# A recurrent attention feeding an MLP: VectorE held to the program's order, weight pieces dealt anew, two turnings set apart

## The chip, the core and the metric

The kernel runs on one core of a Trainium2 chip. A core has several engines that run side by side, each with its own queue of instructions: TensorE (PE, matrix products; its weight loads are shown apart as PEld), VectorE (DVE, elementwise work), ScalarE (ACT, functions of one input and copies), GpSimd (POOL) and SyncE (SP), which here only issues DMAs. An engine works through its queue in order; an instruction whose inputs or buffers are not ready holds up all that stand behind it. The metric is the time of one execution on the device in microseconds (us).

## What is computed

The first half is a gated linear recurrence with 4 batches, 8 heads, 768 steps and a head size of 48. Its output, brought into token order, goes through an MLP with 3072 tokens, 384 in and out, 2048 within.

```python
f = 1.0 / (1.0 + np.exp(-f_logit))
for t in range(S):
    state = f[:, :, t, :, None] * state + np.einsum('bhd,bhe->bhde', k[:, :, t], v[:, :, t])
    y[:, :, t] = np.einsum('bhd,bhde->bhe', q[:, :, t], state)
x = y.transpose(0, 2, 1, 3).reshape(B * S, H * D)
h = x @ w_in
g = h * (1.0 / (1.0 + np.exp(-1.702 * h)))
return g @ w_out
```

## The kernel before

**Units.** The tokens are cut into 12 units of 256 (three to a batch). For each unit, the attention yields x for 256 tokens, and the MLP is run on these one to three units later, so that TensorE always has products of the MLP to do while VectorE and ScalarE prepare the next step of the attention.

**The attention of a unit** avoids the step-by-step loop by a tree: six levels of pairs of blocks within chunks of 64 tokens. A level needs scores (L384, bank "sc" of PSUM), masks put on them by VectorE (L410, "A"), products with the rows of v that belong to the level (L448, "y"), and a multiplication of q and k by the gates of the level (`promote`: L436 and L437 in units 0 to 2, one instruction at L439 from unit 3 on), after which ScalarE sets a half of q or k aside for the next level (L423, "Kc" and "Qc"). GpSimd makes the products of the gates (L376, "tot"). After the levels, k is turned (L505, "tkn", and its copy "kn" L506), the sums of k and v per chunk are formed (L523) and VectorE makes four states one after the other (L538, L540, L543, "st"). Then TensorE multiplies q by the states (L563), ScalarE copies the result out of PSUM ("yT", L571), and DMAs bring it to token order ("xT").

In units 0 to 2 a step handles one level (kind W, six steps), from unit 3 on two levels at once (kind V, three steps). The two turns of k are kind T, the states kind S.

**The beginning of the next unit** has four functions, called within the parts of the present unit: `begin_f` (turn the gate logits, make the sigmoid, load those of the unit after), `begin` (turn q, save its last column on GpSimd, load the next q), `begin_k` (turn k; from unit 3 on also the first copies and the first L439), `begin_gates` (the gate products on GpSimd). For units 0 to 2 a turn is made by TensorE and ScalarE (L339, L342); from unit 3 on by one VectorE instruction (L327), for f followed by the sigmoid on ScalarE. `parts_of` (L817) makes the list of a unit's parts and puts the beginnings of the next unit into it, as parts of kind B or K.

**The MLP.** A group h of 128 hidden columns is three matmuls over 256 tokens (L727); then come the sigmoid on ScalarE (L732) and g on VectorE (L733). There are 16 such groups per unit, in four blocks. The product with w_out is done plainly for units 0 to 2 (L755, added up at L791 and L793), and from unit 3 on by seven products of quarters instead of eight (L704, with banks X, W, Y, Z). For these, VectorE makes sums of quarters of g (L641, L643, L644, L650) and of w_out (L622, once), and combines the products (u, L679 to L691). Matmul results of h, o, and the turns share four banks of PSUM.

**The weights** arrive as bits of another format and are converted by VectorE. There are 32 pieces (half of w_in, half of w_out), and each takes one ScalarE instruction (L208) and five on VectorE (L223, L219, L226, L227, L228, on 128x384 each). `convert()` emits one such instruction. Three buffers hold fetched pairs of pieces; a fetch is issued by SyncE as soon as a pair is done.

**The order.** `merge(n, fill, columns, share, pieces, …)` writes out the order of the work for unit n. It goes through the parts of the unit; after each part it emits a share of MLP work from the list `fill` (shares W 3, V 4, S 3, T 1, B 1, K 1, out of their total, of `columns` columns of matmul in all), and spreads conversions between them until `pieces` pieces are dealt. `UNIT` is the MLP work of a unit, 24576 columns, `DM` is 384, `LAG` is 18 DM. Two scopes say which engines keep this order as written:

```python
ctx.enter_context(tc.manual_schedule(engines={mybir.EngineType.PE}))
fill_order = ExitStack()
fill_order.enter_context(tc.manual_schedule())
...
merge(3, fill, 3 * UNIT // 2 - LAG // 2, steady, 6, by=0.7)
fill_order.close()
```

Up to the end of merge(3) all engines keep the written order; after `fill_order.close()` only TensorE does, and a scheduler orders the instructions of the other engines when the kernel is built.

Of the kernel before, what the change touches and what calls it, by code (L numbers as in the profile page):

```python
# [23 lines left out]
def kernel(  # L24
# [34 lines left out]
    B, H, S, D = q.shape  # L59
    DM = H * D  # L60
# [25 lines left out]
    wp = ctx.enter_context(tc.tile_pool(name="wp", bufs=2))  # L86
    mlp = ctx.enter_context(tc.tile_pool(name="mlp", bufs=2))
    ps = ctx.enter_context(tc.tile_pool(name="ps", bufs=1, space=bass.MemoryType.PSUM))
    ctx.enter_context(tc.manual_schedule(engines={mybir.EngineType.PE}))
    fill_order = ExitStack()  # L90
    fill_order.enter_context(tc.manual_schedule())

# [138 lines left out]
    def convert():  # L231

        if state["begin"] < len(pairs) and len(todo) <= NOP:
            begin_pair(state["begin"])
            state["begin"] += 1
        if todo and todo[0]:
            todo.pop(0)()
        if todo and todo[0] is None:
            todo.pop(0)
            state["done"] += 2  # L240
            fetch_weights()
# [34 lines left out]
    def load_vl(n, l):  # L276

        if n >= NALL:
            return
        t = vls[n, l] = ld.tile([P, DM], F32, tag=f"vl{l}", name=f"vl_{n}_{l}")  # L280
        if n < N_TURN:
            pt = ps.tile([P, DM], F32, tag="mm", name=f"tv_{n}_{l}", bufs=4)
            for g in range(NG):
                nc.tensor.matmul(
                    pt[g * 64:(g + 1) * 64], lhsT=perm[:, l - 1, :] if l else ident[:, ::2], rhs=vns[n][:, g, :],
                    start=True, stop=True,
                )
            nc.scalar.copy(t, pt)
            return
        nc.sync.dma_start(out=t, in_=v_toks[n % 2].rearrange("(n two m) e -> two n m e", two=2, m=LEV[l])[0])  # L290
# [507 lines left out]
    def mlp_blocks(*blocks):  # L798

        hs, os = zip(*(mlp_block(n, r) for n, r in blocks))  # L800
        return sum(hs, []) + sum(os, [])


    def keep_up(times):

        if times:
            pt = ps.tile([P, NL * 64], F32, tag="mm", name=f"idle_{next(serial)}", bufs=4)
        for _ in range(times):
            nc.tensor.matmul(pt, lhsT=ident, rhs=masks.rearrange("p l t -> p (l t)"), start=True, stop=True)

    units = [attention(n) for n in range(NALL)]
    LAG = 18 * DM

    def parts_of(n):

        parts = list(units[n][1])
        _, inter = parts.pop()  # L817
        if n:
            kind, scores = parts[0]
            _, ahead = units[n - 1][1][-1]  # L820
            parts[0] = kind, lambda: (ahead(), scores())
        if n < N_TURN:

            def with_v(l):
                kind, fn = parts[l]
                return kind, lambda: (fn(), load_vl(n, l) if n == 0 or l else None, keep_up(2 * (n == 0 and l < 3)))
            parts[:NL] = [with_v(l) for l in range(NL)]
        if n + 1 < NALL:
            begin_f, begin, begin_k, begin_gates = units[n + 1][0]
            i = len(parts)  # L830
            if n + 1 < N_FILL:

                parts.append(("K", lambda: (begin_k(), begin_gates(), load_vl(n + 1, 0) if n + 1 < N_TURN else None)))
                parts.insert(i - 4, ("B", begin if n == 0 else lambda: None))
                parts.insert(i - 5, ("B", begin_f))
                if n:

                    kind, head = parts[0]
                    parts[0] = kind, lambda: (head(), begin())
            else:  # L840
                kind, states = parts.pop()
                parts += [("B", begin_k), (kind, lambda: (states(), begin_gates()))]
                parts.insert(i - 3, ("B", lambda: (begin_f(), begin())))
        else:
            parts.append(("W", inter))
        return parts

    def merge(n, fill, columns, share, pieces=0, hold=0, by=1.0, chores=()):

        parts = parts_of(n)
        total = sum(share(kind) for kind, _ in parts)
        converting = {"W": 3, "T": 3, "B": 1} if n < N_FILL - 1 else {"W": 3, "V": 4, "S": 3, "T": 1, "B": 1}
        total_ops = sum(converting.get(kind, 0) for kind, _ in parts)
        held = sum(share(kind) for kind, _ in parts[:hold])
        at = at_ops = done = ops = 0
        for kind, fn in parts:
            ready = state["done"]
            fn()  # L860
            for chore in chores[:2]:
                chore()
            chores = chores[2:]
            at += share(kind)
            at_ops += converting.get(kind, 0)
            n_ops = min(int(pieces * NOP * at_ops / (by * total_ops)), pieces * NOP) - ops
            ops += n_ops
            first, n_columns = done, max(0, columns * (at - held) / (total - held) - done)

            def some(end):  # L870
                nonlocal done
                while fill and done < end and fill[0][2] <= ready:
                    w, emit, _ = fill.pop(0)
                    emit()
                    done += w
            for i in range(n_ops):
                some(first + n_columns * i / n_ops)
                convert()
            some(first + n_columns)
# [4 lines left out]
    UNIT = NFF * NK * U + U // P * NFF * DM  # L884
# [12 lines left out]
        load_raw(1, j)  # L897
    load_vn(1)
    fill = []
    merge(0, fill, 0, steady, 8)  # L900
    fill += mlp_blocks((0, 0)) + mlp_blocks((0, 1))
    merge(1, fill, UNIT // 2 - LAG // 2, steady, 10, hold=1)
    fill += mlp_blocks((1, 0), (1, 1)) + mlp_blocks((0, 2), (1, 2))
    merge(2, fill, UNIT, steady, 8)
    fill += mlp_blocks((2, 0), (2, 1)) + mlp_blocks((2, 2), (0, 3)) + mlp_blocks((1, 3), (2, 3))
    merge(3, fill, 3 * UNIT // 2 - LAG // 2, steady, 6, by=0.7)
    fill_order.close()
    for n in range(3, NALL):
        fill += mlp_unit(n)
# [33 lines left out]
```

## Time and profile before

| | us |
|---|---|
| median of 13 runs | 655.84 |
| lowest and highest of them | 654.84, 658.31 |
| the profiled execution, its own time | 655.26 |
| span of that execution in the trace | 653.3 |
| TensorE busy in the span | 632.1 |
| VectorE busy | 445.0 |
| ScalarE busy | 229.9 |
| GpSimd busy | 60.1 |

The profile is of one execution. Its span runs from the first to the last instruction; the execution's own time holds 2.0 us more. TensorE's granted clock was at full speed throughout. Three kinds of view are used. Stage rows give, for a stretch of the span, the busy time of each engine, with the number of instructions in brackets, the granted clock, the mean share of the DMA engines and the rate. Waits give, for an instruction that waited, who released it, then the sum, the number of times, and the longest. Timeline rows give the start, the duration, the engine, the line, the operation, and output and input by the program's names, with their sizes and, in square brackets, the idle time before and its releaser. "x2" means two instructions in one row.

### The profile page before, as it was taken

The numbers are of one execution on the slowest core, as the hardware profiler recorded it, in microseconds if no ns is written. First come the engines' busy times: TensorE is split into PE (matmuls) and PEld (weight loads), VectorE is DVE, ScalarE is ACT, GpSimd is POOL, SyncE is SP. The second block draws the span as 40 slices with busy tenths as digits, with TensorE's granted clock in tenths as the row PEclk, the third lists the DMA queues.
The fourth block names the chain that finished last, engine by engine and source line by source line (L and its number), as shares of the span: only waits on it lengthen the run. The fifth ranks groups of instructions, "written<-read, shape, count | busy, mean of one in ns | idle before, by whom it ended". The sixth has DMA issues, their size and how long they took to land.

```text
span 653.3 us, 20397 instructions
## 1 busy us (share of the span) xinstructions
PE 632.1 (97%) x8958; PEld 541.8 (83%) x8958; DVE 445.0 (68%) x802; ACT 229.9 (35%) x477; POOL 60.1 (9%) x116
## 2 busy tenths in 40 slices
PE   6979999999999999999999999999999999999997
PEld 5656767767768789989989989989989889989997
DVE  2998977788787658558558558559559557553571
ACT  4464444333224324324324324334334333232120
POOL 3050020010001002002002002002002002000000
PEclk9999999999999999999999999999999999999999
DMA  8888874384044634604605605605604202101000
GB/s 193 220 206 214 219 162 122 105 201 79 25 93 122 168 72 121 166 27 122 165 25 129 160 26 128 159 26 130 158 27 108 63 25 64 38 2 26 25 1 24
DMA packets 67554, 67.67 MB, mean 104 GB/s; under 512 B 30410, under 2 KB 61290, under 8 KB 67466
## 3 DMA queue, kind: packets, MB, share of 16 engines
q1 hardware_dynamic: 67466, 66.38, 40.6%
q8 instruction: 70, 1.15, 0.8%
q14 instruction: 18, 0.15, 0.1%
HBM read 56.92 MB, written 8.65 MB: 100 GB/s over the span
## 4 chain that ended last, share of the span: by engine, by line
PE 86%; DVE 9%; ACT 2%; DMA 1%; issue 1%; SPq 1%; DVEq 0%; ACTq 0%
PE h L727 37%; PE o_Y L704 8%; PE o_X L704 7%; PE o L755 7%; PE o_Z L704 7%; PE sc L384 5%; PE y L448 4%; PE o_W L704 4%; PE t L339 2%; PE y L563 2%; PE sc L523 1%; PE tkn L505 1%; DMA xT<-yT 1%; DVE s L219 1%; DVE A L410 1%
## 5 line engine op out<-in xcount | busy, mean ns | idle before, releaser
L727 PE MATMUL h<-xT,w_in 128*128 128x256 f32 (+1 forms) x1152 | 259.8, 381 | 5.1 <-DMA xT<-yT 3.0
L727 PEld LDWEIGHTS h<-xT,w_in 128*128 128x128 f32 x1152 | 215.3, 190 | 38.6 <-issue 4.3
L733 DVE TENSOR_TENSOR g<-h,sg 128x256 f32<-128x256 f32 (+1 forms) x192 | 81.0, 423 | 97.8 <-ACT sg L732 95.4
L732 ACT ACTIVATE sg<-h 128x256 f32<-128x256 f32 (+1 forms) x192 | 73.5, 384 | 192.5 <-PE h L727 187.4
L423 ACT COPY Kc<-X 128x512 f32<-128x512 f32 x69 | 46.2, 669 | 119.3 <-DVE X L439 84.7
L755 PE MATMUL o<-w_out,g 128*128 128x384 f32 x192 | 66.1, 493 | 0.0
L439 DVE TENSOR_TENSOR X<-X,tot 128x1024 f32<-128x1024 f32 x45 | 55.1, 1225 | 15.4 <-PE sc L384 10.2
L755 PEld LDWEIGHTS o<-w_out,g 128*128 128x128 f32 x192 | 35.3, 190 | 22.9 <-issue 1.4
L704 PE MATMUL o_X<-w_out,g 128*128 128x192 f32 x288 | 51.9, 329 | 0.0
L704 PE MATMUL o_Y<-T,S 128*128 128x192 f32 x288 | 51.1, 331 | 0.1
L704 PEld LDWEIGHTS o_Y<-T,S 128*128 128x128 f32 x288 | 46.5, 190 | 2.6 <-DVE u L679 1.2
L704 PEld LDWEIGHTS o_X<-w_out,g 128*128 128x128 f32 x288 | 47.3, 190 | 0.9
L410 DVE TENSOR_TENSOR A<-sc,masks 128x512 f32<-128x512 f32 x72 | 46.8, 681 | 0.0
L376 POOL TENSOR_TENSOR tot<-F 128x512 f32<-128x512 f32 x12 | 12.5, 1042 | 342.3 <-DVE st L540 342.3
L448 PE MATMUL y<-A,vl 64*48 64x64 f32 x2304 | 41.2, 217 | 1.0 <-issue 0.6
L448 PEld LDWEIGHTS y<-A,vl 64*48 64x48 f32 x2304 | 36.2, 120 | 4.5 <-issue 3.8
L327 DVE STREAM_TRANSPOSE X<-raw 128x1024 f32<-128x1024 f32 x18 | 36.7, 2041 | 2.3 <-PE y L563 2.3
L571 ACT COPY yT<-y 48x512 f32<-48x512 f32 x48 | 27.8, 580 | 12.9 <-PE y L563 12.4
L384 PEld LDWEIGHTS sc<-X,Kc 48*64 48x64 f32 x1344 | 24.0, 134 | 8.9 <-issue 3.2
L384 PE MATMUL sc<-X,Kc 48*64 48x64 f32 x1344 | 28.3, 220 | 2.5 <-DVE A L410 2.1
L376 POOL TENSOR_TENSOR tot<-tot 128x256 f32<-128x256 f32 (+4 forms) x60 | 27.4, 457 | 4.7
L357 POOL COPY q_last<-X 128x4 f32<-128x4 f32 x12 | 14.0, 1166 | 141.2 <-DVE X L327 111.3
(93 smaller groups left out, 674.7 us busy)
## 6 DMA issues: line engine op xcount, KB each, us to landing
vl<-v_tok SPq DMA_DIRECT2D x60, 192.0 KB, 3.0
bits<-in_moe_w_out_dram SPq DMA_DIRECT2D x8, 768.0 KB, 10.1
bits<-in_moe_w_in_dram SPq DMA_DIRECT2D x8, 576.0 KB, 8.2
v_tok<-in_v_dram SPq DMA_DIRECT2D x10, 384.0 KB, 4.3
vn<-v_tok SPq DMA_DIRECT2D x10, 384.0 KB, 6.9
xT<-yT SPq DMA_DIRECT2D x24, 144.0 KB, 2.8
raw<-in_q_dram SPq DMA_DIRECT2D x18, 192.0 KB, 3.9
raw<-in_f_logit_dram SPq DMA_DIRECT2D x18, 192.0 KB, 4.7
```

Of the source, the lines that this page charges most:

```text
L327: nc.vector.transpose(out.rearrange("p (a i j) -> p a j i", a=NP, j=R), raw[:, j].rearrange("p a (j d) -> p (a j) d", j=R)[:, :, :32],)
L376: nc.gpsimd.tensor_tensor(tn, t2[:, :, 0], t2[:, :, 1], ALU.mult)
L384: nc.tensor.matmul(out[g * HS:(g + 1) * HS, h, a, :], lhsT=lhs(h, a * U + g * G), rhs=rhs(h, a * U + g * G), start=True, stop=True,)
L410: nc.vector.tensor_tensor(A[:, :, c:c + w].rearrange("p h (x t) -> p h x t", t=64), t["sc"][:, :, c:c + w].rearrange("p h (x t) -> p h x t ...
L423: nc.scalar.copy(c.rearrange("p (n m) -> p n m", m=m), X[:, j, :NA].rearrange("p (n two m) -> p n two m", two=2, m=m)[:, :, hf, :],)
L439: nc.vector.tensor_tensor(qk, qk, by, ALU.mult)
L448: nc.tensor.matmul(dst(h, g, a), lhsT=vls[n, u][g * 64:(g + 1) * 64, (2 * a + h) * D:(2 * a + h + 1) * D], rhs=A(h, g, a), start=(start an ...
L704: nc.tensor.matmul(t[bank], lhsT=lhs(f), rhs=rhs(f), start=(new and f == 0), stop=(f == HF - 1), skip_group_check=True,)
L727: nc.tensor.matmul(ph, lhsT=w_in[:, c, ff * P:(ff + 1) * P], rhs=xTs[n][:, c, :], start=(c == 0), stop=(c == NK - 1))
L732: nc.scalar.activation(sg, ph, AF.Sigmoid, scale=1.702)
L733: nc.vector.tensor_tensor(g[ff // FG][:, ff % FG, :], ph, sg, ALU.mult)
L755: nc.tensor.matmul(t["po"], lhsT=g[ff // FG][:, ff % FG, tt * P:(tt + 1) * P], rhs=w_out[:, ff, :], start=(ff == ffs[0]), stop=(ff == ffs[ ...
```

## The change

Four things are changed.

1. VectorE joins TensorE in the scope that lasts for the whole kernel: after merge(3) its instructions too stand in the order in which the program writes them. ScalarE, GpSimd and SyncE are ordered by the scheduler after merge(3), as they were.
2. From the third merge on (merges 2 to 10, where the next unit is 3 or later), `begin_f` and `begin` are no longer one part. `begin_f` stays where it was, and `begin` becomes a part of its own two places later. The total of the shares in those merges grows by one.
3. The pieces of weights dealt to merges 0 to 3 are 6, 10, 9, 7 instead of 8, 10, 8, 6. Their sum stays 32.
4. merge(1) gets 3·DM = 1152 columns of MLP work less, and merge(3) 1152 more.

```diff
-    ctx.enter_context(tc.manual_schedule(engines={mybir.EngineType.PE}))
+    ctx.enter_context(tc.manual_schedule(engines={mybir.EngineType.PE, mybir.EngineType.DVE}))
...
                 parts += [("B", begin_k), (kind, lambda: (states(), begin_gates()))]
-                parts.insert(i - 3, ("B", lambda: (begin_f(), begin())))
+                parts.insert(i - 3, ("B", begin_f))
+                parts.insert(i - 1, ("B", begin))
...
-    merge(0, fill, 0, steady, 8)
+    merge(0, fill, 0, steady, 6)
     fill += mlp_blocks((0, 0)) + mlp_blocks((0, 1))
-    merge(1, fill, UNIT // 2 - LAG // 2, steady, 10, hold=1)
+    merge(1, fill, UNIT // 2 - LAG // 2 - 3 * DM, steady, 10, hold=1)
     fill += mlp_blocks((1, 0), (1, 1)) + mlp_blocks((0, 2), (1, 2))
-    merge(2, fill, UNIT, steady, 8)
+    merge(2, fill, UNIT, steady, 9)
     fill += mlp_blocks((2, 0), (2, 1)) + mlp_blocks((2, 2), (0, 3)) + mlp_blocks((1, 3), (2, 3))
-    merge(3, fill, 3 * UNIT // 2 - LAG // 2, steady, 6, by=0.7)
+    merge(3, fill, 3 * UNIT // 2 - LAG // 2 + 3 * DM, steady, 7, by=0.7)
     fill_order.close()
```

The number of instructions on each engine stays the same.

## The prediction

> **What bounds the kernel now.** I read first the totals and the forty slices, then busy time by stage, then the waits, then the timeline at one hand-over between units.
>
> ```profile
> PE 632.1 (97%) x8958; PEld 541.8 (83%) x8958; DVE 445.0 (68%) x802; ACT 229.9 (35%) x477; POOL 60.1 (9%) x116
> PE   6979999999999999999999999999999999999997
> DVE  2998977788787658558558558559559557553571
> ```
>
> TensorE works 632.1 of 653.3 us, and the change takes no matmul away. So all that can be won is in its 21.2 us of idle time, and VectorE's row says where: it is full only in the first slices.
>
> ```profile
> core 0: us, PE busy (x) PEld busy (x) DVE busy (x) ACT busy (x) POOL busy (x), PEclk, DMA share, GB/s
> 0.00:56.00 56.00, 43.48 (x962) 32.72 (x964) 40.71 (x96) 27.91 (x50) 16.08 (x38) 1.00 0.84 200
> 56.00:93.00 37.00, 35.45 (x606) 24.77 (x603) 35.01 (x80) 18.52 (x37) 3.64 (x6) 1.00 0.87 214
> 93.00:158.00 65.00, 61.35 (x729) 45.06 (x731) 51.79 (x103) 22.73 (x48) 3.75 (x8) 1.00 0.56 131
> 158.00:246.00 88.00, 88.00 (x1048) 68.11 (x1041) 62.17 (x105) 28.02 (x60) 5.08 (x10) 1.00 0.36 94
> 246.00:600.00 354.00, 353.93 (x5363) 325.17 (x5362) 230.75 (x373) 124.48 (x261) 31.52 (x54) 1.00 0.34 87
> ```
>
> The rows are, in turn, unit 0; unit 1; unit 2 with the start of unit 3; the rest of unit 3 with unit 4; seven steady units. Idle TensorE by subtraction: 12.5, 1.6, 3.7, 0.0, 0.1, and 3.4 in the tail that is left out. From 158 us on there is nothing to win and something to lose: the gain must come out of the first 158 us. The waits name the small ones there, and two that already exist in steady units:
>
> ```profile
> PE h L727 <- DMA xT<-yT: 3.0, 3, 1.3
> PE h L727 <- ACT kn L506: 1.3, 1, 1.3
> PE y L563 <- DVE st L543: 1.2, 3, 0.5
> DVE X L439 <- ACT Qc L423: 6.1, 7, 1.5
> ```
>
> Columns: sum, times, longest. The last two say that the state sums (st) are sometimes just late for TensorE, and that the second score step waits for ScalarE's copies.
>
> **The change part by part.** Counts of instructions stay: order and timing change. The granted clock is 1.00 in every row, so I take all durations as they are.
>
> *Six pieces for eight in unit 0.* A piece costs five VectorE instructions (L223 0.37, L219 0.555, L226 0.35, L227 0.55, L228 0.55 us each; in back-to-back pairs they take about 0.27 and 0.47). Ten instructions fewer are 3.9 to 4.7 us of VectorE, which runs without a break from 13 to 45 us. But the level chain (L436, ScalarE's copy 0.66, scores 0.65, next L436) can't go faster than about 2.2 us a level. Dealing 3, 3, 4, 5, 4 conversions to levels instead of 4, 5, 4, 7, 6, and 10 instead of 14 ahead of the states, I get the states at 38.4 where the trace has them at 41.5: **−3.1 us** at the end of unit 0. If TensorE's own turns of k and v decide instead, −2.3.
>
> *Ten pieces in unit 1, with 1152 columns of MLP less.* The row 56 to 93 shows VectorE full: 35.0 of 37, and 57.4 to 83.9 with 0.6 us of gap. All 50 conversions remain; only one product g (0.42) leaves the stretch ahead of the states. TensorE, however, has two groups of h fewer there (2 × 1.295 = 2.6 us), so it now waits for about 2.2 us. The two groups come back after the states' scores, where they cover the 1.3 us wait for xT in the waits above. At the first h of unit 1 (trace: 92.5 us) I have 90.5, with the same TensorE work done: of −3.1, **−2.0 us** is left.
>
> *Nine pieces for eight and seven for six in units 2 and 3; 1152 columns more in unit 3.* Row 93 to 158 has VectorE at 80%; 10 instructions more at 0.4 are 4 us beside 13 of gap. The small stalls of TensorE at h there (xT 0.47, the sums 0.33, and 0.51 where a g stands behind two sums of w_out, L622, that the scheduler had pulled in) go, but the scores of unit 3 ask for more work in front of them. At those scores (sc of the second pair of levels) I have 37.5 us after h_8 of unit 0's last block, before 37.4: **+0.1**, between −1.2 and +1.5.
>
> *VectorE in program order from unit 3 on.* L622 (7.4 us in all) falls back behind the mark among g_9 to g_11, where TensorE has h in hand; its cost is the delay of one g: **+0.1**. In the tail of unit 3 the turning of F stands between g_12 and g_13: 2.05 us in which no bank of h comes free, with three banks ahead: 0 to 0.9, I take **+0.4**.
>
> *Turnings of f and q.* Today they run right after the states, in the gap before the score steps:
>
> ```profile
> 254.72 2.05 DVE L327 STREAM_TRANSPOSE F<-raw 128x1024 f32<-128x1024 f32 x1 [0.83 <-POOL tot L376]
> 256.62 1.29 DVE L650 TENSOR_TENSOR g<-g,S 128x512 f32<-128x512 f32 x2
> 258.28 2.06 DVE L327 STREAM_TRANSPOSE X<-raw 128x1024 f32<-128x1024 f32 x1 [0.37 <-PE y L563]
> 260.45 1.20 DVE L439 TENSOR_TENSOR X<-X,tot 128x1024 f32<-128x1024 f32 x1
> 261.58 1.27 DVE L410 TENSOR_TENSOR A<-sc,masks 128x512 f32<-128x512 f32 x2
> 263.02 1.24 DVE L439 TENSOR_TENSOR X<-X,tot 128x1024 f32<-128x1024 f32 x1 [0.18 <-ACT Qc L423]
> ```
>
> In the program's order they stand a whole unit's h later: f after g_8, q behind the sums that follow g_11, k after g_14. So the place above becomes free (4.1 us less ahead of L439), and 6 us of turning is put among the products. Behind the f-turning on VectorE wait g_9 and, on ScalarE, sg_10 (behind F's sigmoid, 1.06); TensorE waits for those only when four banks of h are filled. The raw loads on SyncE's queue, and POOL's two q_last copies (L357, 1.17 mean), are issued as much later and are still a unit ahead of use; POOL's own order is the same, as is that of SyncE's outputs; one w_out fetch goes behind an xT transfer, not ahead of it.
>
> Walked from h_8's end at 28.2 us after a score step: f turned 28.97 to 30.85, sigmoid to 32.0, q turned 35.2 to 37.1, k turned from 38.7 (behind g_14), first L439 step 41.45, g_15 42.6, two sums, states 44.4 to **47.5**. TensorE by its own work needs the states at 47.82. So the unit still fits, with about **0.3 us of slack**, where today the turnings are out of this chain altogether. The other place: after the scores, the copies yT (2.37 after y) hold ScalarE's Kc and Qc, so the second L439 starts 2.95 after the scores, u is ready at 6.9, and TensorE wants it at 6.7: 0.22, today 0.04 to 0.27. Score starts move two h-groups earlier (a share of 4/20 for 4/19 of the columns), behind which o_X and o_Y give cover. Starts of y in the trace at 257.16, 306.00, 403.32, 452.07, 500.68, 549.45 give 48.72 us a unit; I get 48.7 to 48.9. I take **0** for the seven hand-overs (below −0.2 × 7 = −1.5, above +0.4 × 7 = 2.8, up to +0.8 × 7 = 5.6 if the chain is a long way out).
>
> *POOL beside VectorE.* POOL's products now fall beside the first L439 step, which today starts after they end:
>
> ```profile
> 253.65 1.04 POOL L376 TENSOR_TENSOR tot<-F 128x512 f32<-128x512 f32 x1 [40.11 <-DVE st L540]
> 254.77 2.60 POOL L376 TENSOR_TENSOR tot<-tot 128x256 f32<-128x256 f32 x5
> ```
>
> The nearest row is 84.84 us in unit 1: two products with both inputs in SBUF beside these same POOL products took 1.12 and 0.88 for 0.68 alone.
>
> ```profile
> 84.84 1.12 DVE L436 TENSOR_TENSOR X<-X,F 128x512 f32<-128x512 f32 x1 [0.25 <-PE sc L384]
> 85.89 0.88 DVE L437 TENSOR_TENSOR X<-X,F 128x512 f32<-128x512 f32 x1
> ```
>
> By the row, at most +0.44 for the step, 0.3 of it hidden by the wait for yT: +0.14 a unit. [...] But at 256.62 two L650, both inputs in SBUF, ran beside tot at 0.65 each, no slower than elsewhere. I take the row, and inside the 0 above.
>
> **Sum:** −2.0 + 0.1 + (0.1 + 0.4) + 0 = **−1.4 us**. The profiled execution took 655.26 us (653.3 span, 2.0 around it), 0.58 below the median of 655.84: from the median, **654.4**.
>
> **The rivals.**
> - *VectorE's queue is late in steady units (slower).* The chain f-turning, q-turning, k-turning, L439, states has 0.3 us of slack on 19. For it: six us of turning now stand in it, and program order can't let g_15 or the states pass a late turning. Against: TensorE's 100% leaves banks free whenever VectorE is 65% busy. It decides once the chain is over 0.3 us longer than walked; 0.4 a unit gives 2.8 + 0.9 + 0.1 − 2.0 = +1.8: 657.6; at 0.8, 660.4.
> - *The front's gain is not kept.* VectorE is full in unit 1, and unit 2 and 3 have ten conversions more: the 3.1 us is given back as waits for h or o on converted weights. 656.0.
> - *More goes than I count.* Stalls in the row 93 to 158 (1.3 us by the waits) and the 0.2 waits at u (1.4 over seven) also go: −2.0 − 1.3 − 1.4 = −4.7: 651.1.
>
> **How the numbers follow.** Forecast 0.44, own range 652.9 to 655.9 (±1.5, the bounds of unit 3 and the tail); late queue 0.32; gain not kept 0.08; more goes 0.16. About 0.2%, 1.3 us, is what can be told from no change here. Faster: 0.29 of the forecast, 0.16, 0.01 = 0.46. Same: 0.13 + 0.02 + 0.03 = 0.18. Slower: 0.02 + 0.30 + 0.04 = 0.36. The range goes from the fourth case to half way between the two prices of the late queue: 651.0 to 659.0.
>
> **What would show it.** The states of unit 0 at about 38.4 us, the first h of unit 1 at 90.5; TensorE idle in unit 1 up by 2 us while unit 0's idle falls by 3; starts of y 48.7 to 48.9 us apart; the first L439 step after y at 1.2 to 1.6 us with POOL beside it; no wait of y for st above 0.5 us. A step of y to y over 49.1 makes the forecast wrong, as does a first h of unit 1 later than 92.

## The result, and the profile after

The changed kernel takes 660.63 us (median of 11 runs, 658.64 to 664.86), the kernel before 655.43 (median of 48, 653.74 to 658.83). The ratio is 1.0089, interval [1.0075, 1.0103]: slower, where 654.4 was forecast. The profiled execution took 660.04 us with a span of 658.3, 5.0 more than the span before. First its page, then the same stage rows as before.

```profile
PE 637.8 (97%) x8958; PEld 544.2 (83%) x8958; DVE 443.6 (67%) x802; ACT 227.2 (35%) x477; POOL 50.7 (8%) x116
```

```profile
0.00:56.00 56.00, 46.87 (x1034) 34.33 (x1034) 40.29 (x93) 29.77 (x53) 10.59 (x38) 0.97 0.87 198
56.00:93.00 37.00, 35.84 (x598) 25.34 (x592) 34.12 (x80) 16.92 (x35) 3.64 (x6) 1.00 0.84 205
93.00:158.00 65.00, 60.78 (x767) 45.03 (x758) 51.29 (x99) 22.65 (x47) 3.95 (x8) 0.95 0.57 145
158.00:246.00 88.00, 87.09 (x954) 66.71 (x953) 60.85 (x108) 26.98 (x59) 3.19 (x8) 1.00 0.30 81
246.00:600.00 354.00, 352.31 (x5337) 321.72 (x5336) 231.30 (x375) 121.97 (x261) 29.32 (x56) 1.00 0.34 88
```

TensorE's idle time is 658.3 − 637.8 = 20.5 us, not more than the 21.2 before. But it is busy for 5.7 us longer with the same 8958 matmuls. The column after POOL says why: the granted clock is 0.97 and 0.95 in two rows where every row before had 1.00. In rows of 3 us, around the products with the states of unit 2:

```profile
128.00:131.00 3.00, 3.00 (x12) 2.12 (x12) 2.04 (x2) 0.92 (x2) 0.00 (x0) 1.00 0.94 231
131.00:134.00 3.00, 0.88 (x3) 0.19 (x1) 2.14 (x4) 1.71 (x5) 0.00 (x0) 1.00 1.06 280
134.00:137.00 3.00, 1.63 (x64) 1.19 (x64) 2.69 (x9) 0.67 (x2) 0.19 (x1) 0.98 1.09 218
137.00:140.00 3.00, 2.81 (x66) 2.42 (x67) 3.00 (x7) 2.32 (x4) 2.69 (x5) 0.50 0.48 124
140.00:143.00 3.00, 3.00 (x6) 1.60 (x5) 2.60 (x4) 0.31 (x1) 0.51 (x2) 0.50 0.52 121
```

TensorE stands, and then gets half its clock until 143.7. TensorE's timeline shows the gap itself (the bracket is the idle time before the row):

```profile
126.71 1.10 PE L523 MATMUL sc<-vn,kn 64*64 64x48 f32 x64
127.74 1.56 PE L727 MATMUL h<-xT,w_in 128*128 128x256 f32 x6
129.14 2.74 PE L755 MATMUL o<-w_out,g 128*128 128x384 f32 x8
134.76 0.32 PE L563 MATMUL y<-X,st 48*48 48x64 f32 x4 [2.88 <-DVE st L543]
135.54 1.45 PE L563 MATMUL y<-X,st 48*48 48x64 f32 x60 [0.46 <-DVE st L543]
137.19 1.13 PE L384 MATMUL sc<-Qc,Kc 48*64 48x64 f32 x32 [0.21 <-DVE st L543]
```

The two score rows around 137 take 1.13 and 1.10 us; at full clock, in the kernel before, 0.69 and 0.68.

Where the 5.0 us came from can be read from the starts of y (L563), if one allows for the columns of MLP work that now come after them (1536 at units 1 and 2, 768 from unit 3 on; a group h of 768 columns takes 1.295 us: in this trace 18 of its matmuls take 4.05 us at 122.24 and six take 1.46 at 119.76, and two groups lie between).

| y of unit | before | after | columns fewer | difference, same work |
|---|---|---|---|---|
| 0 | 41.92 | 39.82 | 0 | −2.1 |
| 1 | 82.99 | 77.90 | 1536 | −2.5 |
| 2 | 138.45 | 134.76 | 1536 | −1.1 |
| 3 | 208.66 | 208.31 | 768 | +0.9 |
| 4 | 257.09 | 256.83 | 768 | +1.0 |
| 11 | 592.03 | 595.75 | 768 | +5.0 |

So there are two losses in this trace: 3.4 us between unit 1 and unit 3, and 4.0 spread evenly over the steady units. From unit 4 to unit 10 y starts 49.20 us apart; before, 48.72. The second trace of the same kernel (e9 below) gives −1.8 at unit 1, +0.4 at unit 3 and +4.9 at unit 11 in the same way: 2.2 and about 4.4.

### The profile page after: what moved, and what is told of

Read it like the earlier page. It is cut to its first block, busy times and chain, and to the rows that moved or that the text cites. A ratio compares the mean times of both kernels' runs of the same rounds, so it can differ in the third digit from the quotient of the medians.

```text
span 658.3 us, 20410 instructions
## 1 busy us (share of the span) xinstructions
PE 637.8 (97%) x8958; PEld 544.2 (83%) x8958; DVE 443.6 (67%) x802; ACT 227.2 (35%) x477; POOL 50.7 (8%) x116
## 4 chain that ended last, share of the span: by engine, by line
PE 83%; DVE 9%; ACT 3%; DMA 2%; issue 1%; SPq 1%; DVEq 0%; ACTq 0%
PE h L727 36%; PE o L755 9%; PE o_Y L704 6%; PE o_X L704 6%; PE o_Z L704 6%; PE sc L384 5%; PE y L448 4%; PE o_W L704 3%; PE y L563 1%; PE tkn L505 1%; DVE X L439 1%; PE sc L523 1%; DMA vn<-in_v_dram 1%; ACT yT L571 1%; DVE st L543 1%
## 5 line engine op out<-in xcount | busy, mean ns | idle before, releaser
L439 DVE TENSOR_TENSOR X<-X,tot 128x1024 f32<-128x1024 f32 x45 | 55.3, 1229 | 63.5 <-PE sc L384 35.8
L755 PE MATMUL o<-w_out,g 128*128 128x384 f32 x192 | 68.0, 505 | 0.9 <-DVE g L733 0.9
L704 PE MATMUL o_X<-w_out,g 128*128 128x192 f32 x288 | 53.8, 331 | 0.0
L704 PE MATMUL o_Y<-T,S 128*128 128x192 f32 x288 | 52.6, 332 | 0.5 <-DVE u L679 0.4
L357 POOL COPY q_last<-X 128x4 f32<-128x4 f32 x12 | 2.9, 238 | 366.8 <-DVE X L327 290.9
L376 POOL TENSOR_TENSOR tot<-tot 128x256 f32<-128x256 f32 (+4 forms) x60 | 30.4, 507 | 4.7
L704 PE MATMUL o_W<-T,g 128*128 128x192 f32 x144 | 24.9, 326 | 0.0
```

What stands on the lines that cost most here:

```text
L439: nc.vector.tensor_tensor(qk, qk, by, ALU.mult)
L704: nc.tensor.matmul(t[bank], lhsT=lhs(f), rhs=rhs(f), start=(new and f == 0), stop=(f == HF - 1), skip_group_check=True,)
L755: nc.tensor.matmul(t["po"], lhsT=g[ff // FG][:, ff % FG, tt * P:(tt + 1) * P], rhs=w_out[:, ff, :], start=(ff == ffs[0]), stop=(ff == ffs[ ...
```

## The experiments

All ratios are to the kernel before, run on the same chip between the others (its median there was 657.5 to 657.8). "y to y" is the mean distance from unit 4 to unit 10 in the run's trace. e9 is the changed kernel once more, as a base for later runs; its 0.67% is a little under the 0.8 to 1.0% expected of it.

| run | VectorE's order | turnings | columns | pieces | us | ratio | y to y |
|---|---|---|---|---|---|---|---|
| before | free | one part | old | old | | 1 | 48.72 |
| changed (e9) | kept | apart | new | new | 662.00 | 1.0067 [1.0044, 1.0089] | 49.27 |
| e1 | free | apart | new | new | 659.48 | 1.0019 [0.9998, 1.0041] | 48.50 |
| e2 | kept | one part | new | new | 662.81 | 1.0092 [1.0059, 1.0125] | 49.91 |
| e3 | kept | apart | new | old | 664.84 | 1.0108 [1.0083, 1.0132] | 49.29 |
| e4 | kept | apart | old | new | 671.36 | 1.0202 [1.0175, 1.0230] | 50.91 |
| e5 | kept | one part | old | old | 671.18 | 1.0203 [1.0171, 1.0235] | 50.37 |
| e6 | free | one part | new | old | 655.20 | 0.9972 [0.9951, 0.9994] | 48.51 |
| e7 | free | one part | old | new | 656.16 | 0.9982 [0.9955, 1.0010] | 48.72 |
| e8 | free | apart | old | old | 657.16 | 0.9997 [0.9977, 1.0018] | 48.71 |
| e12 | free | one part | new | new | 653.21 | 0.9939 [0.9919, 0.9960] | 48.51 |

**One part undone at a time (e1 to e4).** e1 takes VectorE out of the scope again:

```diff
-    ctx.enter_context(tc.manual_schedule(engines={mybir.EngineType.PE, mybir.EngineType.DVE}))
+    ctx.enter_context(tc.manual_schedule(engines={mybir.EngineType.PE}))
```

> The changed kernel with VectorE free again after the third mark (TensorE alone is held to the program's order); split, pieces and columns stay changed. Theory A (late queue: from unit 4 on the turnings stand in front of the states and of u, and cost about 0.5 us a unit over eight units): the steady 4.0 us go, starts of y come back to 48.7 us apart, the rest stays at about +1 us over the kernel before: 656 to 657. Theory B (what is lost is lost in the hand-over from unit 2 to unit 3 alone, by the wait for the states and the halved clock): no gain, 660 to 661. Both expect the wait of 2.9 us for the states of unit 2 and the halved clock behind it to stay.

The steady loss went, down to 48.50, under the kernel before, as theory A has it; y still waits 2.9 us for the states of unit 2, and the work behind it goes at about half its pace up to 146.2 us: the scores take 1.13 and 1.10 us for 0.69 and 0.68, six products with w_out 4.21, where eight take 2.74 ahead of the gap.

```profile
137.65 0.32 PE L563 MATMUL y<-X,st 48*48 48x64 f32 x4 [2.90 <-DVE st L543]
```

The time, 659.48, lies between the two forecasts. Both theories are thus right about their own half: program order costs the steady units, something else the hand-over.

e2 puts the turnings back into one part, e3 the pieces back to 8, 10, 8, 6, e4 the columns back:

```diff
-                parts.insert(i - 3, ("B", begin_f))
-                parts.insert(i - 1, ("B", begin))
+                parts.insert(i - 3, ("B", lambda: (begin_f(), begin())))
```

> The changed kernel with the turnings of f and q back in one part. Theory A: q's turning stands one turn of k earlier, so k's turning and the states come up to 2 us earlier than now; the wait of y for st in steady units (about 0.25) goes, that of u (0.3) stays: 1.5 to 2 us won there. In the hand-over from unit 2 to 3 the wait for the states shrinks from 2.9 to about 1.5, TensorE waits for kn again (1.3), and no gap is long enough for the clock to fall: 3.3 us more. Together 655.5 to 657. If the place of q's turning is of no matter: 660 to 661.

> The changed kernel with the pieces dealt 8, 10, 8, 6 as before. Unit 0 loses the 2 to 3 us that six pieces gave (first states at about 41 us, not 38). If the five conversions more in unit 2 make its states late, the wait of 2.9 falls by about 2 us, the clock stays up, and the time comes out at 657 to 659; if they do not, it stays and the time is 662 to 664.

> The changed kernel with the MLP columns of units 1 and 3 as before (1152 back ahead of the second mark). Theory B (TensorE came to the states of unit 2 with 2.6 us less of MLP work in hand, stood 2.9 us, and got half its clock for 6.7 us): the wait falls to about 0.3 us, the clock stays full there, and 5 us less the 1 to 2 us that unit 1 loses are won: 656 to 657.5. Theory A: the steady 4.0 us remain in the trace, with y 49.2 us apart. If neither the wait nor the clock falls in with the columns, 660 to 661.

e2 missed: its steady units are 0.7 us worse than those of the changed kernel. Two turnings in a row keep VectorE from every g for 4 us (one takes 2.04 in the changed kernel's trace), and h finds no bank (h waits for g in six steady units, 0.7 us each). In unit 2, however, y waits only 0.19 us before the first state, and TensorE waits 2.26 at kn instead; a fall of 3.4 us followed all the same. e3 came in at 664.84, just over the upper of its two figures: y still waits 2.1 us in unit 2, so the conversions alone don't make the gap. e4 missed most: the wait in unit 2 fell only to 1.9 us, the clock still fell, and the steady units became far worse, 50.91. With VectorE's order fixed, 768 columns more or fewer ahead of y decide what stands in front of what: o_X waits for ScalarE's copies (L669) up to 1.1 us, seven times in the steady units. By y to y, under program order the moved columns save 1.6 us a unit and the set-apart turnings 0.6.

**One part alone (e5 to e8)**, each the same edit made to the kernel before.

> The kernel before with one edit: VectorE in the program's order to the end. The trace of the changed kernel with old columns loses 2.1 us in each steady unit against the kernel before, that with one turning 1.2. Theory A' (program order alone costs most, and the split turnings and the moved columns are what makes it bearable): both losses come together, 2 to 3 us a unit, +16 to +24 us: 673 to 681. Rival (the losses come from single parts and don't add): +1 to +2.1 a unit, 665 to 673.

> The kernel before with the columns alone moved (1152 fewer in unit 1, more in unit 3). Steady units: 48.5 us from y to y as in the run with VectorE free, so 1.4 to 1.6 us won there. Front: TensorE has 2.6 us less work in hand at the states of unit 2, waits up to 2.9 us for them, and the clock falls for 3.4 or 6.8 us (1.7 or 3.4 us lost): 2 to 4 us lost. Together +0.5 to +2.5 over the kernel before. If the columns have no part in the front's loss: -1.5.

> The kernel before with the pieces alone dealt 6, 10, 9, 7. By the prediction's first two steps the states of unit 0 come 2 to 3 us earlier, of which 1.5 to 2 are left at the end of unit 1; steady units as before: -1 to -2. If the conversions that are moved into units 2 and 3 make the states of unit 2 late (a wait over 2 us and a fallen clock behind it): 0 to +3.

> The kernel before with the turnings of f and q apart, VectorE free after the third mark. Steady units: a scheduler orders VectorE there, so only the share of columns moves: within 0.2 us a unit. In unit 2, where the written order holds, q's turning comes later, TensorE waits less for kn (1.3 before) and more for the states: 0 to +2 with the clock up, +3.4 more if it falls.

Order alone costs 2.0%, within the range of the rival, so the losses of e2 and e4 don't simply add. Columns alone gain 0.28%: the steady units win 0.21 us each as expected, and the loss feared for the front did not come (longest wait for states 0.5). Pieces alone may gain (−0.18%, an interval that takes in 0). The turnings alone do nothing that can be told (interval −0.23 to +0.18%).

**Both gains together (e12), and the gap itself (e10, e13).**

> The kernel before with the moved columns and the pieces 6, 10, 9, 7, but VectorE free after the third mark and the turnings in one part. If the two gains (0.28% and 0.18%) add: 0.4 to 0.5% faster than before. If they meet in unit 2 (TensorE 2.6 us further ahead, VectorE with five conversions more), the states of unit 2 are waited for by over 2 us and the clock falls there: -0.1% to +0.2%, as in the run with VectorE free and the turnings apart.

They add: 653.21 us, 0.61% under the kernel before, the best version here. The meeting in unit 2 that the second figure feared did not come: y waits 0.20 us there before the first state:

```profile
136.92 0.32 PE L563 MATMUL y<-X,st 48*48 48x64 f32 x4 [0.20 <-DVE st L543]
```

Between e12 and e1 stand only the turnings set apart, which do nothing alone (e8), yet e1 is 0.8% slower. e13 asks whether it is their place in unit 2. It is the changed kernel with this:

```diff
-                parts.insert(i - 3, ("B", begin_f))
-                parts.insert(i - 1, ("B", begin))
+                if n == 2:
+                    parts.insert(i - 3, ("B", lambda: (begin_f(), begin())))
+                else:
+                    parts.insert(i - 3, ("B", begin_f))
+                    parts.insert(i - 1, ("B", begin))
```

> The changed kernel with the turnings of f and q in one part while unit 2 runs, apart from unit 3 on. Theory C (in unit 2, where VectorE still converts weights, q's turning set later pushes the states behind TensorE; the gap and the halved clock follow): the wait for the states of unit 2 falls from 2.9 to below 1.2, no clock of one half behind it, and 3 to 5 us come off the changed kernel: 0.0 to +0.3% over the kernel before, the steady units at 49.2 us as they are. Rival (the gap comes from columns and pieces, whatever the turnings do): 0.7 to 1.0% as now.

659.67 us, 1.0037 [1.0013, 1.0062], y to y 49.28. TensorE's timeline of e13:

```profile
126.48 4.15 PE L727 MATMUL h<-xT,w_in 128*128 128x256 f32 x18 [2.27 <-ACT kn L506]
...
133.47 2.74 PE L755 MATMUL o<-w_out,g 128*128 128x384 f32 x8
136.41 0.32 PE L563 MATMUL y<-X,st 48*48 48x64 f32 x4 [0.19 <-DVE st L543]
137.19 1.45 PE L563 MATMUL y<-X,st 48*48 48x64 f32 x60 [0.46 <-DVE st L543]
138.85 0.69 PE L384 MATMUL sc<-Qc,Kc 48*64 48x64 f32 x32 [0.21 <-DVE st L543]
```

The gap at the states is gone, and an earlier one of 2.27 us, at the copy kn, has taken its place. So the wait was moved, not made: with q's turning later, TensorE passes kn sooner and stands at the states instead, nearly as long. But behind the gap at kn the clock stays full, and scores take 0.69 us. In the trace that is worth 3.4 us. By the ratios it is 0.3% against e9, where the intervals overlap, and 0.5% against the first comparison, where they don't.

e10 leaves the changed kernel as it is and gives TensorE something to do in the gap:

```diff
             py = t["py"]
+            for _ in range(5 * (n == 2)):
+                nc.tensor.matmul(
+                    py[:NP, 0, :, 1::2], lhsT=q_last[-1], rhs=masks[:, :4],
+                    start=False, stop=True, skip_group_check=True,
+                )
```

> The changed kernel with five matmuls of zeros (256 columns each, added to y's bank, so no value changes) put in front of the products with the states of unit 2, where TensorE otherwise stands for 2.9 us. Nothing else moves: the states come at the same time. Theory C (the gap costs twice: once as a wait, and once more because it makes the clock fall): the clock stays at 1.00 after it and 3.4 us come off the changed kernel's time, 0.5% of it. Rival (the clock falls for another reason, the load of the stretch for one): no change, or up to 0.5 us slower.

660.18 us, 1.0045 [1.0021, 1.0069], against 1.0067 of e9 beside it. First e9, the changed kernel, then e10, in rows of 3 us:

```profile
131.00:134.00 3.00, 1.43 (x5) 0.54 (x3) 1.69 (x2) 1.71 (x5) 0.00 (x0) 1.00 1.04 311
134.00:137.00 3.00, 1.36 (x36) 1.15 (x40) 2.62 (x8) 1.22 (x4) 0.00 (x0) 0.70 1.09 215
137.00:140.00 3.00, 3.00 (x101) 2.88 (x98) 2.96 (x7) 1.84 (x4) 2.42 (x4) 0.50 0.69 139
140.00:143.00 3.00, 3.00 (x7) 1.69 (x7) 3.00 (x5) 0.48 (x1) 0.97 (x3) 0.66 0.33 78
```

```profile
131.00:134.00 3.00, 3.00 (x11) 1.51 (x10) 1.71 (x2) 1.22 (x2) 0.00 (x0) 1.00 0.90 258
134.00:137.00 3.00, 2.32 (x14) 0.78 (x11) 2.30 (x6) 2.11 (x5) 0.00 (x0) 1.00 1.07 237
137.00:140.00 3.00, 2.21 (x96) 1.94 (x100) 2.83 (x7) 1.02 (x2) 1.21 (x2) 0.87 0.96 206
140.00:143.00 3.00, 3.00 (x43) 2.14 (x38) 3.00 (x8) 1.30 (x3) 2.18 (x5) 0.56 0.49 129
```

Half the effect came. The fall lasts 3.4 us in e10, 6.8 in e9; the products of zeros end at 136.0, 0.67 us before the states, and the short waits between the states (0.46, 0.21) follow. The medians differ by 1.8 us, about one fall of 3.4 us at half speed, though the two intervals overlap; the mean clock over the runs rose from 0.993 to 0.996. So the falls became fewer or shorter over the runs, but the full 3.4 us were not won, and one trace each doesn't show that the work in the gap did it. The added matmuls, on tiles of 128x4 where those of h have 128x128, take 2.32 us in the trace of e10.

**The steady 0.5 us (e11, e14).** e11 moves q's turning one part sooner; e14 takes one sum out of the chain in front of the states:

```diff
-                parts.insert(i - 1, ("B", begin))
+                parts.insert(i - 2, ("B", begin))
```

```diff
-            tt(g[j][:, :, t1], g[j][:, :, t1], g[j + 2][:, :, t1], ALU.add)
+            if b == 2:
+                tt(g[j][:, :, t1], g[j][:, :, t1], g[j + 2][:, :, t1], ALU.add)
```

> The changed kernel with q's turning one part sooner (directly after the part of f's, a twentieth of the columns apart). In the changed trace ScalarE's copy of Qc waits 1.5 us for q's turning and the two copies of GpSimd behind it, with the sigmoid of h_14 queued behind, and so k's turning is 0.4 us later than I walked. Theory A (that 0.4 is what makes y wait for the states): the wait of about 0.2 us at y goes, a steady unit gains 0.2, 1.5 us in all, or 0.2% off the changed kernel. Rival (turnings so close together hold up g, as in the run with one part, where h waited for g 0.7 us in each unit): 0.2 to 0.7 us a unit are lost, +0.2 to +0.8%.

> The changed kernel without the first of the two sums of g that stand in front of the states (L643 after h_15: the second half of g's columns is not added up, so the output differs in that part), 0.69 us of VectorE less in each unit from 3 on. Theory A (the chain turnings, L439, g, sums, states has no slack): y waits for the states no longer, 0.25 to 0.35 us a unit, 2 to 2.8 us in all, 0.3 to 0.4% off the changed kernel. If the wait at u alone makes the steady loss: within 0.1% of the changed kernel.

e11 went the rival's way: 662.97 us, 1.0087 [1.0056, 1.0118], y to y 49.82, h waiting for g up to 0.7 us in six units. The waits of y for the states are gone from its steady units, as theory A had it, but those of h cost more. None of the three places tried for q's turning under program order is good: sooner it blocks g, later it delays k's. It made the gap in unit 2 shorter (1.3 us, a fall of 3.4 us only), which agrees with theory C. e14: 660.21 us, 1.0045 [1.0015, 1.0074], y to y 48.97. Of 0.69 us taken out of the chain, 0.23 a unit came back, 1.9 us over eight units, a little under what was expected. In weight loads, the wait of the scores behind y (1.5 us) is gone, those of y for the states are 1.6 us in all (1.9 before the edit), and u's grew from 2.4 to 3.4. So the chain makes about half of the 0.48; that the other half is u's is read from the waits and wasn't tried by itself.

## Why the prediction was wrong

**Unit 0: right.** The states were forecast for 38.4 us; they start at 38.58 (before, 41.52).

**Unit 1: the right place, a size too small.** I had TensorE wait 2.2 us there for VectorE and −2.0 left; the row 56 to 93 has 1.2 us idle in all, the wait for xT is gone, and the first h of unit 1 starts at 89.67 (forecast 90.5, before 92.54). So the forecast wait for VectorE did not come. The profiled run also had a first fall of the clock, 3.4 us long, at 14.0 us. It seems to have cost nothing: e9's profile of the same kernel is without it, yet has its first h of unit 1 at 90.23 and a span of 658.2 us.

**The step that failed first: "The granted clock is 1.00 in every row, so I take all durations as they are."** I priced idle time as itself. From unit 1 to unit 3, TensorE's idle time rose only from 3.65 to 4.22 us in the row 93 to 158; my +0.1 for that stage (bounds −1.2 and +1.5) held for the waits. But 1.3 at kn and some small ones became one gap of 2.9, then half the clock for 6.8 us: 3.4 us, as much as the table shows between y of unit 1 and unit 3. I also wrote that no wait of y would be above 0.5; I had followed VectorE's chain there against TensorE's old pace, and TensorE came with 1536 columns less in hand and with 0.5 us of waiting for kn in place of 1.3. The gap needs the set-apart turning of q, and the other parts add to it: 0.2 us without that turning (e12, e13), 1.1 with it alone (e8), 1.95 without the moved columns (e4), 2.1 without the new pieces (e3), 2.9 with all.

**The second: 0 for the seven hand-overs, with 0.3 us of slack.** The rival of the late queue had the mechanism, and its price of 0.4 a unit was close: 0.48 measured, over eight units rather than seven. (The starts of y that I listed are 0.07 to 0.11 us later than the trace has them; their distance, 48.72, is right.) The walk was right to 0.1 us as far as q's turning, and then 0.4 late. VectorE and ScalarE in a steady unit of the changed kernel; the scores before it end at about 259.7, so q's turning was due at 294.9, k's at 298.4, the states at 304.1:

```profile
294.84 2.04 DVE L327 STREAM_TRANSPOSE X<-raw 128x1024 f32<-128x1024 f32 x1
296.94 0.19 POOL L357 COPY q_last<-X 128x4 f32<-128x4 f32 x1 [34.55 <-DVE X L327]
297.42 0.66 ACT L423 COPY Qc<-X 128x512 f32<-128x512 f32 x1 [1.46 <-POOL X L358]
297.98 0.65 ACT L732 ACTIVATE sg<-h 128x256 f32<-128x256 f32 x2
298.39 0.42 DVE L733 TENSOR_TENSOR g<-h,sg 128x256 f32<-128x256 f32 x1 [0.93 <-ACT sg L732]
298.73 2.06 DVE L327 STREAM_TRANSPOSE X<-raw 128x1024 f32<-128x1024 f32 x1
...
304.51 0.35 DVE L540 TENSOR_TENSOR st<-st,tot 128x192 f32<-128x192 f32 x1
```

ScalarE's copy Qc waits 1.46 us for q's turning and then for GpSimd's two copies into X; the sigmoid of h_14 stands behind it on ScalarE, g_14 behind that, and k's turning behind g_14. I had called GpSimd's copies harmless because they are a unit ahead of their use, and missed that Qc reads the tile they write. By the timeline, this ate the slack. The other half of the loss is at u, which I had walked to a wait of 0.22 and priced at nothing, since up to 0.27 of it was there before. Weight loads in steady units, before and then after:

```profile
PEld o_Y L704 <- DVE u L679: 1.2, 4, 0.3
```

```profile
PEld o_Y L704 <- DVE u L679: 2.4, 7, 0.5
...
PEld sc L384 <- PE y L563: 1.5, 5, 0.3
PEld y L563 <- DVE st L543: 1.2, 5, 0.3
PEld y L563 <- DVE st L540: 0.7, 3, 0.2
```

**The sum.** Forecast were −2.0 up to unit 1, +0.6 from there to unit 4 and 0 for the steady units: −1.4. The table has −2.5, +3.5 and +4.0: +5.0. Of the difference of 6.4 us, 4.0 are the second step and 2.9 the first one (3.4 by the clock, less what was won beside it); unit 1 gave 0.5 more than forecast.

**The rest.** The turning of F in the tail of unit 3 cost its upper bound (o waits 0.9 us for a g, at 186.1). GpSimd beside VectorE: the first L439 step after the hand-over at 306 us took 1.23 us with GpSimd's five products beside it, no more than any of the 45 of them before (1.20 to 1.24), while those products took 3.07 us for 2.60.

```profile
308.54 3.07 POOL L376 TENSOR_TENSOR tot<-tot 128x256 f32<-128x256 f32 x5
309.14 1.23 DVE L439 TENSOR_TENSOR X<-X,tot 128x1024 f32<-128x1024 f32 x1 [1.47 <-PE sc L384]
```

So this step was not held up, where the row of unit 1 (1.12 and 0.88 us for 0.68) had let me allow up to 0.44 for it; it was GpSimd's products that took 0.47 us longer, less than the length of the step.

**The rivals.** That of the late queue was right in kind and, at 657.6, short by 3.0 us, about what the clock took. "The front's gain is not kept" was wrong as far as unit 1, where −2.5 was won; the gain went at unit 2, to the clock and not to waits on converted weights. "More goes than I count" holds for a kernel that isn't this one: with the columns moved and VectorE free, the waits at u do go (none in e12's steady units, 48.51 a unit).

## What to carry to other kernels

A gap of TensorE had two prices here: its length, 2.9 us at the states of unit 2, and 6.8 us of half clock behind it. Several short waits and one long one of the same sum were not the same: 1.3 us at kn and 0.2 at the states, in the kernel before, had a clock of 1.00 behind them. Before a wait is moved, ask whether it joins another, and read in the trace what the clock does behind the place that it goes to: 2.27 us at kn in e13 left it full, 2.9 at the states did not. And where an engine is put into program order, look at what stands behind a waiting instruction, on the other engines too: ScalarE's copy Qc, 1.46 us late here, held up g_14 on VectorE by 0.93 and k's turning behind it. Follow each output of a moved instruction to all of its readers, small ones included, before calling the slack positive.

## What had not been expected of the hardware

The clock falls to 0.50 and stays there for 3.4 us or 6.8 us, in the changed kernel's trace from 13.99 to 17.41 and from 136.87 to 143.70. That costs up to 1.7 or 3.4 us (an estimate, the half of each). What brings a fall these runs don't show. Over the states of unit 2, the gap of TensorE in front of the first product with them, and the fall beside it:

| run | gap, us | us at half clock there |
|---|---|---|
| changed, e9, e14 | 2.88, 2.88, 2.90 | 6.8 |
| e1 | 2.90 | about half pace from 140.1 to 146.2, by the rows |
| e3 | 2.08 | 4.9 or more |
| e4 | 1.95 | 6.7 or more |
| e11 | 1.31 | 3.4 |
| e8 | 1.10 | none |
| e10 | 0.67 | 3.4 |
| e6 | 0.52 | none |
| e5, before, e12, e13 | 0.21, 0.20, 0.20, 0.19 | none |
| e2 | 0.19 | 3.4 |
| e7 | none | none |

The length of a gap thus doesn't decide by itself: 1.31 us (e11) and 0.67 (e10) went with a fall and 1.10 (e8) did not, and 0.19 did in e2 and not in e13. In e14 the fall began 0.8 us before the gap ended, in the changed kernel's first trace 2.1 us after. Gaps of 2.20 to 2.27 us at kn had no fall behind them before the states in e2, e7, e12 and e13. They stand between matmuls on 128x128 tiles, the turns of k and h; behind the gap at the states stand those of y on 48x48 and the scores on 48x64. Whether the tiles are what matters is a guess from these traces; no run varied tiles or gaps by themselves.

The falls differ from execution to execution (the one at 13.99 us is not in e9's trace of the same kernel), and the kernel before scatters too. In 72 of its runs beside e5 to e14, those with a mean clock of 1.000 have a median of 655.5 us (11 runs), with 0.997 657.4 (20), with 0.995 658.1 (22), with 0.992 659.7 (8): some 0.5 us for each thousandth. Its mean clock there is 0.996, the changed kernel's 0.992 in the first comparison. (There the kernel before had a median of 655.43; its clocks in those runs are not on record.) Falls before 100 us stand in 10 of the 15 profiles other than e1's; the one that I predicted from had a clock of 1.000, which was luck. In the mean over runs the clock therefore costs the changed kernel some 2 us against the kernel before (an estimate, four thousandths at 0.5), not 3.4. At the same clock it is slower all the same: with 0.992 its runs, e9's among them, have a median of 662.1 (9 runs) against 659.7.
